# A transformer block on one core: four GpSimd weight scalings and five output stores moved to other places of a hand-written order

## The chip, the cores and the metric

The program runs on one core of one Trainium2 chip. The metric is the device time of one execution in microseconds (us). The kernel before the change was timed three times: median 263.94 us, 263.94 to 264.63. Engines are named as in the profile: PE is TensorE (PEld its weight loads), DVE VectorE, ACT ScalarE, POOL GpSimd, SP SyncE; a q behind the name (SPq, ACTq) means the engine's own instruction queue, where its DMAs are issued.

## What is computed

The block has S = 2048 rows of width D = 448. `c` is one row that modulates both halves. Cut to what matters here:

```
sa, ca, ga, sb, cb, gb = split(silu(c) @ w_mod)
h = layernorm(x) * (1 + ca) + sa
x = x + ga * (linear_attention(h) @ wo)        # 16 heads, softmax feature maps
h = layernorm(x) * (1 + cb) + sb
z = gelu(h @ w_in)                             # 1792 wide
z1, z2 = z[:, :896], layernorm(z[:, 896:])
g = w_sp @ z2 + b_sp                           # 2048 x 2048, over the rows
x = x + gb * ((z1 * g) @ w_out)                # w_out is 896 x 448
```

The gates `ga` and `gb` are multiplied into the rows of `wo` and `w_out` on the chip, once, so that no gate is applied to an output.

## The kernel before, in words

The work is cut into 16 tiles of 128 rows. `fast_path` runs no loops over stages. Instead a string, `ORDER`, lists every step by name, with its tile numbers, its PSUM slot behind `@` and its engine behind `/` (V is DVE, S is ACT, G is POOL, Y is SP). The last loop of `fast_path` (lines 1146 to 1158) reads the string word by word and emits the step. Every engine executes its own instructions in the order in which they were emitted, and waits on semaphores where an operand comes from elsewhere. So the string fixes the order on each engine, and the DMAs of a step marked Y stand in SP's queue in that order too. A PSUM slot (A0, A1, A2 of two banks, B0, B1 of one) is reused only after the last reader of its former content.

The steps that the change and the prediction touch:

- `wos:k` and `wts:k` (`gate_rows`, line 937) multiply one 448-wide row block of `wo` (four blocks, f_wo) or of `w_out` (seven blocks, f_wout) by the gate in f_g_rep, in place. `wts:4`, `wts:3` on POOL and `wts:5` on DVE stay where they are.
- `kP:i` (line 886) normalises the key features, on DVE or POOL; `kA` (line 896) sums keys times values on PE.
- The attention's second half, per tile i: `nM` on PE (numerator and denominator into a slot, line 948), `nX` on ACT and `nC` on DVE (line 959, reads PSUM), then for a pair of tiles `nS` on DVE, three instructions on SBUF data: f_dn add (line 963), its reciprocal (964) and the weights f_w (965). `nT:i` on DVE (968) multiplies the numerator out of PSUM by the weights and is the last reader of the slot; `nA:i` on DVE or POOL (974) adds the two halves into f_opad; `T2` on SP transposes f_opad into f_oT; `wM` and `wN` on PE (984) multiply by `wo`.
- `qM:n` on PE (line 920) makes the query features of the following tiles. `qM:5` takes slot A1 after `nM:0`, so it waits for `nT:0`. `nM:2` takes A0 after `nM:1`, so it waits for `nT:1`.
- `SHw` on PE (767) reads f_win, then `SCw` scales f_win in place, on POOL (773), DVE (775) or ACT (771).
- `T3` on SP (1022) transposes the second LayerNorm's output into f_hT, which `zM` (1028) and `yM` (1056) on PE read; `W` on SP (1064) loads a transposed piece of w_sp.
- `zN:i` (1050) normalises z2, on DVE or POOL; all 16 tiles of it feed `gM` on PE (1072), whose result `gG` on DVE (1078, 1079) joins with z1.
- `oM:t` on PE (1085) multiplies tile t by all seven blocks of f_wout; `oE:t` on DVE (1088) adds x, and `oD:t` on SP (1107) stores 112 KB of output. The last tile, 15, is done in two column parts: `oN`, `oF:15,0` and `oF:15,1` (1100), then `oG:15,0` stored from SP and `oG:15,1` from ACT (1104).

Of the kernel before, what the change touches and what calls it, by code (L numbers as in the profile page):

```python
# [498 lines left out]
T2:0,1 W:0,6 nT:1 SCw:3,1/G SCw:1,1/G SCw:0,2/V SCw:0,3/V SCw:2,1/V nA:1/G T2:1,2 qE:3 qM:4@A2 qM:5@A1 qF:4 qE:4 nM:2@A0 nM:3@A2 nX:2 nC:2 nX:3 nC:3
nS:1 qF:5 nT:2 nT:3 qE:5 wN:0@B0 wR:0/S SB@B1 nM:4@A1 nM:5@A0 bz/S nX:4 nX:5 nC:4 nC:5 nS:2 nA:2/G nT:4 nA:3/G nT:5 nA:4/G wN:1@B0 wQ:0/S wR:1/S  # L500
wQ:1/S SCw:2,0/S l2R:0,2/G l2r:0,2 l2a:0/G SCw:0,0/V nA:5/V T2:2,4 T2:4,6 qM:6@A2 nM:6@A1 nM:7@A0 wN:2@B0 wN:3@B1 qE:6 nX:6 nC:6 nX:7 nC:7 nS:3 nT:6
nT:7 qF:6 wR:2/S wQ:2/S wR:3/S wQ:3/S l2R:2,4/V nA:6/G nA:7/G l2r:2,4 l2a:3/G l2a:2/G qM:7@A2 nM:8@A1 nM:9@A0 wN:4@B0 wM:5@B1 W:1,1 T3:0,1 T2:6,8 qE:7
nX:9 nC:9 nX:8 qF:7 zM:0@A2 wR:4/S gt zG:0 nC:8 l2a:1/V nS:4 nT:8 nT:9 T3:1,2 wR:5/V nM:10@A1 nX:10 wM:6@B0 wQ:4/V wR:6/V SCw:1,0/G SCw:3,0/G wQ:5/S
l2R:4,6/G l2r:4,6 l2a:4/G nM:11@A0 nX:11 nC:10 nC:11 zQ:0/S zM:1@A2 zG:1 zQ:1/S zR:0,2/G zW:0,2 nA:8/V nS:5 nA:9/V nT:10 T3:2,4 wM:7@B0 wR:7/V l2a:5/V
W:1,5 T2:8,10 T3:4,6 yM:0,0@B1 zM:2@A2 zM:3@A1 yG:0,0 wQ:6/S zG:2 zG:3 nT:11 nM:12@A0 nM:13@A2 wQ:7/V zN:0/V zN:1/V nX:12 wM:8@B0 wM:9@B1 nC:12 nX:13
nC:13 zQ:3/S zQ:2/S zM:4@A1 nA:10/V nS:6 wR:8/V nA:11/G nT:12 nT:13 wR:9/V nA:12/V nA:13/V l2R:6,8/G l2r:6,8 l2a:6/G l2a:7/G T2:10,12 wQ:8/S wQ:9/V
zR:2,4/G zW:2,4 yM:0,1@B0 l2R:8,10/G l2r:8,10 l2a:8/G l2a:9/G zG:4 yG:0,1 zQ:4/S zN:2/V zN:3/V zM:5@A0 nM:14@A2 nM:15@A1 wN:10@B0 wN:11@B1 zG:5 nX:14
nX:15 nC:14 nC:15 nS:7 wR:10/S wQ:10/V nT:14 nT:15 nA:14/V nA:15/V wR:11/S zQ:5/S zR:4,6/G zW:4,6 T3:6,8 zM:6@A0 zG:6 wQ:11/S zQ:6/S T2:12,14 W:1,0
wM:12@B0 wM:13@B1 zM:7@A2 l2R:10,12/V yM:0,4@A1 yM:1,4@A0 l2r:10,12 l2a:11/G T3:8,10 T2:14,16 zG:7 zQ:7/S zN:4/V zN:5/V zR:6,8/G zW:6,8 wR:13/V yG:0,4
wQ:13/S zM:8@A2 zM:9@A1 l2a:10/V wR:12/V wM:14@B0 wM:15@B1 wQ:12/V l2R:12,14/V W:1,3 T3:10,12 W:2,1 l2r:12,14 l2a:12/G zN:6/V zN:7/V yG:1,4 zG:8 zG:9  # L510
# [7 lines left out]
guard@A0 gM:1,5@B1 oM:1,0,7@A2 oE:1 oE:2 oE:3 gM:1,2@A0 gG:1,2 gM:1,1@B0 gM:1,3@A2 gM:1,0@A1 gG:1,3 gG:1,0 gM:1,6@A2 oD:0/Y oD:3/Y oD:2/Y gG:1,1
gG:1,5 gG:1,6 gM:2,0@B0 yM:2,2@B1 yG:2,2 W:3,0 W:3,3 W:3,7 W:3,1 W:3,6 W:3,4 W:3,2 gM:2,2@A2 gG:2,0 oM:6,0,7@B0 gM:2,3@B1 oM:4,0,7@A1 gM:2,5@A0 oE:4
gG:2,5 gG:2,3 gM:2,6@A1 gG:2,6 gG:2,2 oM:5,0,7@B1 oE:5 oE:6 gM:2,4@A0 gM:2,1@B0 gG:2,1 oM:7,0,7@B1 oE:7 W:3,5 oD:1/Y gM:3,3@A2 read gG:2,4 oM:8,0,7@B0  # L520
oE:8 oM:10,0,7@B1 oM:9,0,7@B0 oE:9 oE:10 oD:8/Y oD:10/Y oD:6/Y oD:5/Y gM:3,2@A1 gM:3,5@B0 gM:3,1@B1 gG:3,1 gG:3,2 gM:3,6@A0 gM:3,4@B1 gG:3,6 gG:3,4
# [685 lines left out]
```

## Time and profile before

| what | value |
|---|---|
| median of 3 runs | 263.94 us |
| the profiled execution's own time | 263.43 us |
| span of the profiled execution | 261.6 us |
| PE busy | 250.9 us, 96% |
| DVE busy | 158.3 us, 61% |
| POOL busy | 88.9 us, 34% |
| wts and wos on POOL | 6 of 1.16 us, 4 of 1.12 us in the mean |

The span goes from the first to the last instruction in the trace; the execution's own time lies 1.8 us above it. A row of a timeline gives the start, the duration, the engine, the line, the operation, the tiles written and read, and in brackets how long the engine sat idle before it and what ended that. A row that ends in x2 or x8 merges instructions. A matmul's end is modelled and lies a little behind the start of the next. A row of the chain of waits gives start, duration and what the end of the program was waiting for at that moment.

### The profile page before, as it was taken

How to read it: one execution, taken by the hardware profiler on the slowest of the kernel's cores; microseconds unless marked ns; L12 is line 12 of the kernel's file. 1: busy time of each engine (PE TensorE's matmuls, PEld its weight loads, DVE VectorE, ACT ScalarE, POOL GpSimd, SP SyncE). 2: the span in 40 equal slices, each digit the busy share in tenths (PEclk: the TensorE clock that was granted, in tenths of full speed). 3: DMA queues.
4: the chain of work that ended last, by engine and by line, in shares of the span. 5: the costliest groups of instructions: out<-in, count | busy, mean ns of one | idle time of the engine just before them, and what ended most of it. 6: DMA issues, size and time to landing. Idle time of an engine off the chain costs nothing.

```text
span 261.6 us, 4387 instructions
## 1 busy us (share of the span) xinstructions
PE 250.9 (96%) x1654; PEld 136.0 (52%) x1663; DVE 158.3 (61%) x358; ACT 110.1 (42%) x224; POOL 88.9 (34%) x149
## 2 busy tenths in 40 slices
...
GB/s 170 269 295 134 212 136 214 204 249 69 62 120 122 105 131 128 157 154 186 109 3 0 1 0 3 18 3 75 0 3 176 122 0 3 18 105 3 0 38 64
DMA packets 68799, 25.23 MB, mean 96 GB/s; under 512 B 58273, under 2 KB 68642, under 8 KB 68770
## 3 DMA queue, kind: packets, MB, share of 16 engines
...
## 4 chain that ended last, share of the span: by engine, by line
PE 84%; DVE 8%; DMA 3%; issue 1%; POOL 1%; ACT 0%; SPq 0%; DVEq 0%
PE g_ps L1072 37%; PE z_ps L1056 9%; PE o_ps L1085 8%; PE z_ps L1028 8%; PE v_ps L873 4%; PE k_ps L865 4%; DVE f_t L968 3%; PE kvacc L896 3%; PE q_ps L920 3%; PE x_ps L984 3%; DMA f_hT<-f_xpad 2%; DMA f_wq_raw<-in_A_wqkv_dram 2%; PE num L948 2%; PE sh_ps L762 1%; DVE f_dn L963 1%
## 5 line engine op out<-in xcount | busy, mean ns | idle before, releaser
L1072 PEld LDWEIGHTS <-f_z2n 128*128 128x128 bf16 x560 | 50.2, 98 | 46.9
L1078 DVE TENSOR_TENSOR f_gb<-g_ps,f_bsp 128x512 f32<-128x512 f32 (+2 forms) x35 | 20.4, 582 | 55.8 <-PE g_ps L1072 53.6
L1072 PE MATMUL g_ps<-f_Eq,f_z2n 128*128 128x512 bf16 x218 | 49.0, 379 | 0.3
L1059 ACT ACTIVATE f_z1T<-z_ps,f_zb 128x512 bf16<-128x512 f32 x28 | 18.1, 682 | 59.8 <-PE z_ps L1056 59.8
L1028 PE MATMUL z_ps<-f_win,f_hT 112*128 112x448 bf16 (+1 forms) x128 | 26.2, 352 | 0.8 <-DMA f_hT<-f_xpad 0.8
L1056 PE MATMUL z_ps<-f_hT,f_win 112*128 112x512 bf16 x112 | 26.0, 379 | 0.0
L1072 PE MATMUL g_ps<-f_hT,f_z2n 128*128 128x384 bf16 (+1 forms) x224 | 25.1, 272 | 0.0
L1072 PE MATMUL g_ps<-f_wsp,f_z2n 128*128 128x512 bf16 x109 | 24.5, 379 | 0.2
L1085 PE MATMUL o_ps<-f_wout,f_z1T 128*128 128x448 bf16 x105 | 21.7, 352 | 0.1
L1079 DVE TENSOR_TENSOR f_z1T<-f_gb,f_z1T 128x512 bf16<-128x512 f32 (+2 forms) x35 | 20.5, 585 | 1.5
L1088 DVE TENSOR_TENSOR f_xpad<-o_ps,f_x 128x448 bf16<-128x448 f32 x15 | 9.0, 620 | 20.0 <-PE o_ps L1085 20.0
L1028 PEld LDWEIGHTS <-f_hT 112*128 112x128 bf16 (+1 forms) x128 | 12.3, 97 | 13.0 <-DMA f_hT<-f_xpad 1.3
L925 ACT ACTIVATE f_Eq<-q_ps 112x1024 bf16<-112x1024 f32 x16 | 16.1, 1027 | 4.9 <-PE q_ps L920 4.8
L868 ACT ACTIVATE f_E<-k_ps 128x448 bf16<-128x448 f32 x32 | 15.9, 550 | 4.3 <-PE k_ps L865 2.5
L1056 PEld LDWEIGHTS <-f_win 112*128 112x128 bf16 x112 | 10.9, 98 | 12.8
L879 DVE TENSOR_REDUCE f_ksum<-f_E 128x32 f32<-128x896 bf16 x16 | 16.7, 1060 | 0.8 <-ACT f_E L868 0.8
L968 DVE TENSOR_TENSOR f_t<-num,f_w 128x896 bf16<-128x896 f32 x16 | 16.8, 1084 | 0.4
L1032 ACT ACTIVATE f_z2g<-z_ps 128x896 bf16<-128x896 f32 x16 | 14.7, 917 | 4.2 <-PE z_ps L1028 4.0
L920 PE MATMUL q_ps<-f_hT,f_Wq 113*128 113x512 bf16 (+1 forms) x64 | 15.2, 379 | 0.6 <-DVE f_t L968 0.6
L1085 PEld LDWEIGHTS <-f_z1T 128*128 128x128 bf16 x105 | 10.2, 98 | 9.5
L873 PE MATMUL v_ps<-f_wv,f_hT 113*128 113x448 bf16 (+1 forms) x64 | 14.6, 352 | 0.0
L865 PE MATMUL k_ps<-f_Wk,f_hT 113*128 113x448 bf16 (+1 forms) x64 | 14.4, 352 | 0.0
...
## 6 DMA issues: line engine op xcount, KB each, us to landing
out_dram<-f_xpad SPq DMA_DIRECT2D x15, 112.0 KB, 1.8
...
```

What stands on the lines that cost most here:

```text
L865: nc.tensor.matmul(t[:, 0, 0:D], lhsT=hT[0:KR[m], i, m, :], rhs=Wk[0:KR[m], m, :], start=(m == 0), stop=(m == KC - 1))
L873: nc.tensor.matmul(t[:, 0, 0:D], lhsT=hT[0:KR[m], i, m, :], rhs=wv[0:KR[m], m, :], start=(m == 0), stop=(m == KC - 1))
L879: nc.vector.tensor_reduce(out=ksum[:, i], in_=Er[i % NR][:].rearrange("p s (c f h) -> p (s c) h f", c=4, h=HP), axis=AX.X, op=ALU.add)
L920: nc.tensor.matmul(t[:, u, :], lhsT=Wq[0:KR[m], m, cc * CB:cc * CB + P], rhs=hT[0:KR[m], 4 * st:4 * st + 4, m, :], start=(m == 0), stop=(m ...
L968: nc.vector.tensor_tensor(out=tr[i % 2][:], in0=numv(i)[:, :, :, 0:DH], in1=wr[i // 2 % 2][:, i % 2].unsqueeze(3).to_broadcast([P, 2, H, D ...
L1028: nc.tensor.matmul(t[:, hf, 0:D], lhsT=hT[0:KR[m], i, m, :], rhs=win_s[0:KR[m], m, FH + hf * D:FH + (hf + 1) * D], start=(m == 0), stop=(m ...
L1056: nc.tensor.matmul(t[:, 0, :], lhsT=win_s[0:CB, m, fc * P:(fc + 1) * P], rhs=hT[0:CB, 4 * st:4 * st + 4, m, :], start=(m == 0), stop=(m == ...
L1059: nc.scalar.activation(out=stage_b()["z1T"][:, fc, st * 512:(st + 1) * 512], in_=ps["y%d_%d" % (st, fc)][:, 0, :], func=ACT.Gelu_apprx_tan ...
L1072: nc.tensor.matmul(g[:, 0, 0:b - a], lhsT=later["z2n"][:, s_, fc * P:(fc + 1) * P], rhs=wspT[t][:, s_, a:b], start=(s_ == 0), stop=(s_ == ...
L1078: nc.vector.tensor_tensor(out=gb, in0=ps["G%d_%d" % (ch, fc)][:, 0, 0:b - a], in1=bsp[:, t * TCHF + a:t * TCHF + b], op=ALU.add)
L1079: nc.vector.tensor_tensor(out=z, in0=gb, in1=z, op=ALU.mult)
L1085: nc.tensor.matmul(ps["o" + str(t)][:, 0, 0:D], lhsT=later["z1T"][:, fc, t * P:(t + 1) * P], rhs=wout_s[:, fc, :], start=(fc == 0), stop=( ...
```

## The change

Only the string `ORDER` changes. `wts:0`, `wts:6`, `wts:2` and `wts:1` go from between the three `wos` to a place behind `zN:14/G`, much later in POOL's order. `oD:9`, `oD:11`, `oD:12`, `oD:13` and `oD:14` are written further ahead, and `oG:15,0` before `oF:15,1`. All other words keep their order; most of the diff is the string's line breaks. Its core (long lines that only break elsewhere are left out):

```
-kE:13 kS:12 kR:12 kP:12/G kS:13 kR:13 kP:13/G vM:11@B0 vC:11 kA:10@A0 kM:14@B1 kE:14 kF:14 wts:0/G wos:1/G wts:6/G wos:2/G wts:2/G wts:1/G wos:3/G
+kE:13 kS:12 kR:12 kP:12/G kS:13 kR:13 kP:13/G vM:11@B0 vC:11 kA:10@A0 kM:14@B1 kE:14 kF:14 wos:1/G wos:2/G wos:3/G kA:11@A0 kS:14 kR:14 kP:14/V
...
-yM:1,6@B0 yG:0,3 yG:1,6 yM:1,0@A0 yG:1,0 yG:3,6 yM:3,3@A1 yM:0,5@B0 yG:0,5 yG:3,3 yG:0,6 zR:14,16/V zW:14,16 zN:14/G zN:15/V gM:0,6@B1 gM:0,3@B0
+yM:1,6@B0 yG:0,3 yG:1,6 yM:1,0@A0 yG:1,0 yG:3,6 yM:3,3@A1 yM:0,5@B0 yG:0,5 yG:3,3 yG:0,6 zR:14,16/V zW:14,16 zN:14/G wts:0/G wts:6/G wts:2/G wts:1/G
+zN:15/V gM:0,6@B1 gM:0,3@B0 gG:0,3 gM:0,4@A2 gG:0,6 gM:0,2@B0 yM:2,4@B1 yM:2,6@A1 yG:2,6 yG:2,4 gG:0,4 gG:0,2 yM:3,5@A2 yM:3,1@B0 yM:2,3@B1 yG:3,5
...
-gG:3,3 gG:3,5 oD:7/Y gM:3,0@A1 oM:11,0,7@B1 gM:4,2@B0 oD:4/Y gG:3,0 oM:12,0,7@A2 oE:11 oE:12 oM:13,0,7@B1 oE:13 gG:4,2 oD:9/Y gM:4,6@A2 gM:4,4@A1
-gM:4,3@B0 gM:4,0@B1 gG:4,4 gG:4,3 gG:4,0 gM:4,1@A1 gM:4,5@B0 hint oM:14,0,7@B1 gG:4,1 gG:4,6 gG:4,5 oN:15,0@B0 oN:15,1@A1 oE:14 oF:15,0 oF:15,1
-oD:12/Y oD:13/Y oD:14/Y oD:11/Y oG:15,0/Y oG:15,1/S
+gG:3,3 gG:3,5 oD:7/Y gM:3,0@A1 oM:11,0,7@B1 gM:4,2@B0 oD:4/Y gG:3,0 oM:12,0,7@A2 oE:11 oE:12 oD:9/Y oD:11/Y oD:12/Y
+oM:13,0,7@B1 oE:13 oD:13/Y gG:4,2 gM:4,6@A2 gM:4,4@A1 gM:4,3@B0 gM:4,0@B1 gG:4,4 gG:4,3 gG:4,0 gM:4,1@A1 gM:4,5@B0 hint oM:14,0,7@B1 gG:4,1 gG:4,6
+gG:4,5 oN:15,0@B0 oN:15,1@A1 oE:14 oD:14/Y oF:15,0 oG:15,0/Y oF:15,1 oG:15,1/S
```

What it does to POOL's order at the end of the key stage, before and now (line 886 is kP, f_wout rows are wts, f_wo rows wos, line 773 SCw, line 974 nA; a row with x2 or x3 stands for that many):

```order
 L886 TENSOR_TENSOR f_phik<-f_E_129,f_kr_135 128x896
-L937 TENSOR_TENSOR f_wout<-f_wout,f_g_rep 128x448
-L937 TENSOR_TENSOR f_wo<-f_wo,f_g_rep 112x448
-L937 TENSOR_TENSOR f_wout<-f_wout,f_g_rep 128x448
-L937 TENSOR_TENSOR f_wo<-f_wo,f_g_rep 112x448
-L937 TENSOR_TENSOR f_wout<-f_wout,f_g_rep 128x448 x2
-L937 TENSOR_TENSOR f_wo<-f_wo,f_g_rep 112x448
+L937 TENSOR_TENSOR f_wo<-f_wo,f_g_rep 112x448 x3
 L773 TENSOR_SCALAR f_win<-f_win,f_cb_81 112x896 x2
 L974 TENSOR_TENSOR f_opad<-f_t_110 128x4x112
```

Between the last kP and the first SCw there were seven scalings, and now there are three.

POOL's last work of the program, behind the last two `zN` that it executes (f_z2n rows; line 1014 is the power that `zN` needs, line 1119 reads a flag for a branch), as it stands now:

```order
L937 TENSOR_TENSOR f_wout<-f_wout,f_g_rep 128x448
L1014 TENSOR_TENSOR f_zv<-f_zv,f_mhalf 128x2 [waits DVE_49]
L1050 TENSOR_SCALAR f_z2n<-f_z2g_1288,f_zm,f_zv 128x896 [waits DMAHW5_49,Activation_49,Pool_49]
L1014 TENSOR_TENSOR f_zv<-f_zv,f_mhalf 128x2 [waits DVE_49]
L1050 TENSOR_SCALAR f_z2n<-f_z2g_1289,f_zm,f_zv 128x896 [waits Activation_49,Pool_49]
L937 TENSOR_TENSOR f_wout<-f_wout,f_g_rep 128x448 x4
L1119 TENSOR_LOAD flag [waits DVE_49]
```

The four scalings are new there; before, the flag read came right behind the last f_z2n row. The four have no wait of their own.

The last stores in SP's queue. Of the words of the string only `oD:11` changes its place among SP's own instructions: the sequence was 9, 12, 13, 14, 11, then `oG:15,0`, and is now 9, 11, 12, 13, 14, then `oG:15,0`. The rows name no tile, so the change shows only in their waits (line 1107 is oD, line 1104 oG):

```order
 L1107 DMA out_dram<-f_xpad 128x448 [waits DMAHW2_49,DVE_49]
 L1107 DMA out_dram<-f_xpad 128x448 [waits DMAHW3_49,DVE_49]
-L1107 DMA out_dram<-f_xpad 128x448 [waits DMAHW4_49]
+L1107 DMA out_dram<-f_xpad 128x448 [waits DMAHW4_49,DVE_49]
 L1104 DMA out_dram<-f_xpad 128x256 [waits DMAHW5_49,DVE_49]
```

The last `oD` row was tile 11's, which needed no wait for DVE behind tile 14's; it is now tile 14's, which waits for its own `oE:14`. SP issues as many stores as before.

More of the change, by code (lines that the diff above doesn't have):

```diff
@@ L499 @@
[L499 to L510, printed above, removed]
@@ L511 @@
-zQ:8/S W:1,4 zM:10@A2 zM:11@A1 zQ:9/S zR:8,10/G zW:8,10 zG:10 zG:11 zQ:11/S wR:14/V l2a:13/V T3:12,14 W:2,3 W:2,7 wR:15/V wQ:14/V wQ:15/V l2R:14,16/V
+kE:13 kS:12 kR:12 kP:12/G kS:13 kR:13 kP:13/G vM:11@B0 vC:11 kA:10@A0 kM:14@B1 kE:14 kF:14 wos:1/G wos:2/G wos:3/G kA:11@A0 kS:14 kR:14 kP:14/V
+vM:12@B0 kM:15@A2 vC:12 kF:15 kE:15 vM:13@B1 vC:13 kA:12@A0 kS:15 kR:15 kP:15/V vM:14@B0 kA:13@A0 vM:15@B1 vC:14 vC:15 kA:14@A0 csB@B0 kA:15@A0 esB
+KV:0/V KV:1/V KZ:0 KZ:1 qM:3@A2 ccB@B0 nM:0@A1 nM:1@A0 ecB qF:3 nX:0 SHw:3@B0 SHw:2@B1 nX:1 nC:0 nC:1 nS:0 nT:0 nA:0/V T2:0,1 W:0,6 nT:1 SCw:3,1/G
@@ new lines @@
+SCw:1,1/G SCw:0,2/V SCw:0,3/V SCw:2,1/V nA:1/G T2:1,2 qE:3 qM:4@A2 qM:5@A1 qF:4 qE:4 nM:2@A0 nM:3@A2 nX:2 nC:2 nX:3 nC:3 nS:1 qF:5 nT:2 nT:3 qE:5
+wN:0@B0 wR:0/S SB@B1 nM:4@A1 nM:5@A0 bz/S nX:4 nX:5 nC:4 nC:5 nS:2 nA:2/G nT:4 nA:3/G nT:5 nA:4/G wN:1@B0 wQ:0/S wR:1/S wQ:1/S SCw:2,0/S l2R:0,2/G
+l2r:0,2 l2a:0/G SCw:0,0/V nA:5/V T2:2,4 T2:4,6 qM:6@A2 nM:6@A1 nM:7@A0 wN:2@B0 wN:3@B1 qE:6 nX:6 nC:6 nX:7 nC:7 nS:3 nT:6 nT:7 qF:6 wR:2/S wQ:2/S
+wR:3/S wQ:3/S l2R:2,4/V nA:6/G nA:7/G l2r:2,4 l2a:3/G l2a:2/G qM:7@A2 nM:8@A1 nM:9@A0 wN:4@B0 wM:5@B1 W:1,1 T3:0,1 T2:6,8 qE:7 nX:9 nC:9 nX:8 qF:7
@@ new lines @@
+zM:0@A2 wR:4/S gt zG:0 nC:8 l2a:1/V nS:4 nT:8 nT:9 T3:1,2 wR:5/V nM:10@A1 nX:10 wM:6@B0 wQ:4/V wR:6/V SCw:1,0/G SCw:3,0/G wQ:5/S l2R:4,6/G l2r:4,6
+l2a:4/G nM:11@A0 nX:11 nC:10 nC:11 zQ:0/S zM:1@A2 zG:1 zQ:1/S zR:0,2/G zW:0,2 nA:8/V nS:5 nA:9/V nT:10 T3:2,4 wM:7@B0 wR:7/V l2a:5/V W:1,5 T2:8,10
+T3:4,6 yM:0,0@B1 zM:2@A2 zM:3@A1 yG:0,0 wQ:6/S zG:2 zG:3 nT:11 nM:12@A0 nM:13@A2 wQ:7/V zN:0/V zN:1/V nX:12 wM:8@B0 wM:9@B1 nC:12 nX:13 nC:13 zQ:3/S
+zQ:2/S zM:4@A1 nA:10/V nS:6 wR:8/V nA:11/G nT:12 nT:13 wR:9/V nA:12/V nA:13/V l2R:6,8/G l2r:6,8 l2a:6/G l2a:7/G T2:10,12 wQ:8/S wQ:9/V zR:2,4/G zW:2,4
@@ new lines @@
+yM:0,1@B0 l2R:8,10/G l2r:8,10 l2a:8/G l2a:9/G zG:4 yG:0,1 zQ:4/S zN:2/V zN:3/V zM:5@A0 nM:14@A2 nM:15@A1 wN:10@B0 wN:11@B1 zG:5 nX:14 nX:15 nC:14
+nC:15 nS:7 wR:10/S wQ:10/V nT:14 nT:15 nA:14/V nA:15/V wR:11/S zQ:5/S zR:4,6/G zW:4,6 T3:6,8 zM:6@A0 zG:6 wQ:11/S zQ:6/S T2:12,14 W:1,0 wM:12@B0
+wM:13@B1 zM:7@A2 l2R:10,12/V yM:0,4@A1 yM:1,4@A0 l2r:10,12 l2a:11/G T3:8,10 T2:14,16 zG:7 zQ:7/S zN:4/V zN:5/V zR:6,8/G zW:6,8 wR:13/V yG:0,4 wQ:13/S
+zM:8@A2 zM:9@A1 l2a:10/V wR:12/V wM:14@B0 wM:15@B1 wQ:12/V l2R:12,14/V W:1,3 T3:10,12 W:2,1 l2r:12,14 l2a:12/G zN:6/V zN:7/V yG:1,4 zG:8 zG:9 zQ:8/S
@@ L512 @@
+W:1,4 zM:10@A2 zM:11@A1 zQ:9/S zR:8,10/G zW:8,10 zG:10 zG:11 zQ:11/S wR:14/V l2a:13/V T3:12,14 W:2,3 W:2,7 wR:15/V wQ:14/V wQ:15/V l2R:14,16/V
 yM:1,2@B0 zM:12@A2 zM:13@A1 yG:1,2 zG:12 yM:1,3@B0 yM:0,2@B1 yM:2,1@A2 yM:2,5@A0 zQ:10/V zN:8/V zN:9/V zR:10,12/V l2r:14,16 l2a:14/V l2a:15/V zG:13
```

14 lines of the change are left out of this document (6 added, 8 removed).

## The prediction

> **What bounds the kernel now.** I read the page's busy line and its chain by engine first, then the chain of waits in order of time, then the timelines of DVE, POOL and PE side by side where the chain leaves PE, and at last the stores at the end.
>
> ```profile
> PE 250.9 (96%) x1654; PEld 136.0 (52%) x1663; DVE 158.3 (61%) x358; ACT 110.1 (42%) x224; POOL 88.9 (34%) x149
> ...
> PE 84%; DVE 8%; DMA 3%; issue 1%; POOL 1%; ACT 0%; SPq 0%; DVEq 0%
> ```
>
> PE does most of the time on the chain and the change takes no work from it. A gain can come only where the chain is elsewhere: 8% on DVE, 3% on DMA, and what follows the last matmul. The chain of waits leaves PE for DVE once, for a long stretch:
>
> ```profile
> 56.24 0.88 PE num L948 x16
> 57.14 0.20 ACT f_Sx L956
> 57.36 0.20 DVE f_cr L959
> ...
> 79.63 0.59 PE num L948 x8
> ```
>
> From 57.36 to 79.63 us DVE, not PE, is late nearly everywhere; this is the first division by the denominators, and POOL's seven moved or kept scalings end just there. DVE's timeline of it:
>
> ```profile
> 57.59 0.80 DVE L963 TENSOR_TENSOR f_dn<-f_cr 128x32 f32<-128x32 f32 x1
> 58.81 1.01 DVE L965 TENSOR_TENSOR f_w<-f_Sx,f_dn 128x64 f32<-128x64 f32 x1
> 59.85 1.09 DVE L968 TENSOR_TENSOR f_t<-num,f_w 128x896 bf16<-128x896 f32 x1
> 60.98 0.39 DVE L974 TENSOR_TENSOR f_opad<-f_t 128x448 bf16<-128x448 bf16 x1
> 61.29 1.08 DVE L968 TENSOR_TENSOR f_t<-num,f_w 128x896 bf16<-128x896 f32 x1
> 64.23 0.19 DVE L963 TENSOR_TENSOR f_dn<-f_cr 128x32 f32<-128x32 f32 x1
> 64.84 0.23 DVE L965 TENSOR_TENSOR f_w<-f_Sx,f_dn 128x64 f32<-128x64 f32 x1
> 67.42 0.93 DVE L963 TENSOR_TENSOR f_dn<-f_cr 128x32 f32<-128x32 f32 x1
> ```
>
> The same add of 128x32 numbers takes 0.19 us at 64.23 and 0.80 at 57.59 and 0.93 at 67.42; the weights take 0.23 or 1.01. POOL's rows at the slow ones:
>
> ```profile
> 57.31 1.02 POOL L937 TENSOR_TENSOR f_wo<-f_wo,f_g_rep 112x448 bf16<-112x448 bf16 x1
> 58.73 1.01 POOL L773 TENSOR_SCALAR f_win<-f_win,f_cb 112x896 bf16<-112x896 bf16 x1 [0.39 <-PE sh_ps L767]
> 66.27 2.03 POOL L974 TENSOR_TENSOR f_opad<-f_t 128x448 bf16<-128x448 bf16 x2 [2.78 <-DVE f_t L968]
> ```
>
> POOL's instructions end at 58.33, 59.74 and 68.30; DVE's slow ones end at 58.39, 59.82 and 68.35. So a DVE instruction with two SBUF operands, issued while a POOL instruction runs, ends 0.05 to 0.08 us behind it: it waits for POOL. f_t, with one operand in PSUM, takes its 1.09 and 1.08 beside POOL and does not wait.
>
> **The change, first place: the key stage's end.** `wos:3` stood last of seven scalings and ended at 58.33. With four gone before it, POOL's work behind kP ends about four scalings earlier, near 54.4, and POOL then waits for PE's sh_ps, which frees SCw at 58.73 as now (its bracket names PE). So f_dn finds POOL idle at 57.59: 0.80 - 0.19 = 0.61 saved. f_w then starts at 58.20 and ends at 58.43, before SCw starts at 58.73: 1.01 - 0.23 = 0.78 saved. `nT:0` ends at 59.55 in place of 60.94, 1.39 earlier. What is late next is PE:
>
> ```profile
> 58.46 1.90 PE L920 MATMUL q_ps<-f_hT,f_Wq 113*128 113x512 bf16 x8
> 61.00 1.91 PE L920 MATMUL q_ps<-f_hT,f_Wq 113*128 113x512 bf16 x8 [0.64 <-DVE f_t L968]
> 62.74 1.00 PE L948 MATMUL num<-f_KVbd,f_Eq 112*128 112x120 bf16 x16
> 65.86 1.00 PE L948 MATMUL num<-f_KVbd,f_Eq 112*128 112x120 bf16 x16 [0.39 <-ACT f_Eq L925]
> ```
>
> `qM:5` at 61.00 idles 0.64 us for `nT:0`. That idle goes, and no more: `qM:4`'s eight matmuls must be through. From start to start eight of them take 62.74 - 61.00 = 1.74, so `qM:5` may come at 58.46 + 1.74 = 60.20, 0.80 earlier. The gain here is therefore 0.64 to 0.80 of the 1.39, and I take 0.7. `nM:2` follows `qM:5` at 62.0 and needs `nT:1`, and with it `nX:2`, DVE's next `nC` and every later pair move up together. `nT:1` is behind `nA:0`, which has two SBUF operands and comes at 59.6, while the first SCw runs to 59.74. f_w was let in between the two SCw at 59.74 in the row above, so I let `nA:0` in there too: it ends at 60.1 and `nT:1` at 61.2, in time. If it has to wait for the second SCw too, to 60.74, `nT:1` ends near 62.1, and the gain is 0.55. The transposition behind `nA:0` is no limit either:
>
> ```profile
> 61.40 1.19 SPq L847 DMA_TRANSPOSE f_oT<-f_opad  x1
> ...
> f_oT<-f_opad SPq DMA_TRANSPOSE x1, 2.4
> ```
>
> It lands 2.4 us after 61.40, at 63.8, just when `wN:0` now needs it; from 60.1 it lands at 62.5, from 61.1 at 63.5, and 0.3 of waiting there would be lost in the 0.39 that PE waits at 65.86 anyway. From 62 to 79.63 every instruction of the chain waits on the one before, on PE, DVE, ACT and POOL alike, so the shift arrives at PE's long busy stretch. Bounds: 0.8 above; below, 0 if the shift is used up on the way, by more waiting for POOL elsewhere.
>
> **Second place: behind the last zN.** Four scalings, uncontended, cost what `wts:3` costs:
>
> ```profile
> 114.25 1.03 POOL L937 TENSOR_TENSOR f_wout<-f_wout,f_g_rep 128x448 bf16<-128x448 bf16 x1
> 125.26 1.32 POOL L1050 TENSOR_SCALAR f_z2n<-f_z2g,f_zm,f_zv 128x896 bf16<-128x896 bf16 x1
> 137.43 0.69 DVE L1078 TENSOR_TENSOR f_gb<-g_ps,f_bsp 128x512 f32<-128x512 f32 x1 [11.73 <-PE g_ps L1072]
> ...
> 163.14 2.81 PE o_ps L1085 x14
> ```
>
> 4 x 1.03 = 4.1 us from 126.58 to 130.7. DVE is idle from 125.70 to 137.43, so nothing waits for POOL there. The first reader of these blocks is o_ps at 163.14, 32 us later; the new wait of its matmuls on POOL is met long before. Behind the four on POOL stands only the flag read, which waits for a DVE result of the late program. Cost 0; without that cover, had they ended after 163.14, their whole lateness would count.
>
> **Third place: the end.** The last rows of the timeline, with the times to landing of a store that is alone (the one issued at 249.31) and of the last two:
>
> ```profile
> 249.31 0.33 SPq L1107 DMA_DIRECT2D out_dram<-f_xpad  x1
> ...
> 255.35 0.62 DVE L1088 TENSOR_TENSOR f_xpad<-o_ps,f_x 128x448 bf16<-128x448 f32 x1 [0.55 <-PE o_ps L1085]
> 256.00 1.32 SPq L1107 DMA_DIRECT2D out_dram<-f_xpad  x2
> 256.11 0.43 DVE L1100 TENSOR_TENSOR f_xpad<-o_ps,f_x 128x256 bf16<-128x256 f32 x1
> 256.69 0.36 DVE L1100 TENSOR_TENSOR f_xpad<-o_ps,f_x 128x192 bf16<-128x192 f32 x1 [0.15 <-PE o_ps L1096]
> 257.08 0.38 ACTq L1104 DMA_DIRECT2D out_dram<-f_xpad  x1
> 257.42 0.38 SPq L1104 DMA_DIRECT2D out_dram<-f_xpad  x1
> ...
> out_dram<-f_xpad SPq DMA_DIRECT2D x1, 112.0 KB, 1.7
> ...
> out_dram<-f_xpad SPq DMA_DIRECT2D x1, 64.0 KB, 2.7
> ...
> out_dram<-f_xpad ACTq DMA_DIRECT2D x1, 48.0 KB, 2.5
> ```
>
> SP issues tile 14's store at 256.00 and tile 11's behind it, so `oG:15,0`, ready at 256.54, is issued at 257.42 and lands at 257.42 + 2.7 = 260.12, the last event but the closing 1.5 us of the span. ACT's half lands at 257.08 + 2.5 = 259.58. Now tile 11's store goes ahead of tile 12's, and `oG:15,0` can be issued at 256.6, 0.85 earlier; it lands at 259.3 at its 2.7. Then ACT's half is last, at 259.58: a gain of 0.54. It will also land sooner, since 112 KB less is under way; at the lone store's 1.7 it would land at 258.78, a gain of 1.34. I take 0.75, nearer to the row of the same store. Below: if the half lands as late as 3.0 after issue, nothing is gained.
>
> The Trainium skill (DMA: Bandwidth & Descriptors, Anatomy of one DMA) puts a transfer at about 2.0 us fixed plus its bytes over 436 GB/s, fitted on another issue path. By it ACT's 48 KB land 2.1 us after issue, the last term would be 0.94, and the sum 1.64; it would also give a lone 112 KB store 2.26 us, where the trace shows 1.7, so I stay with the rows.
>
> **The sum.** 0.7 + 0 + 0.75 = 1.45 us. The profiled execution took 263.43 us with a span of 261.6; it comes to 261.98 (span 260.15). The median of the runs lies 0.51 above the profiled one: 263.94 - 1.45 = 262.5 us. Bounds of this case: 0.55 + 0.54 = 1.1 to 0.8 + 1.34 = 2.1, so 261.8 to 262.85.
>
> **The rivals.**
>
> *The first stage gives nothing*: f_dn and f_w are short again, but the shift is eaten by later waits between DVE and POOL, as the one at 67.42. For it: nine tenths of a microsecond can go by one bad overlap. Against: the later POOL steps wait for the same DVE results and move with them. 263.94 - 0.75 = 263.2.
>
> *The end gives nothing*: the landing of ACT's half grows to 3 us. For it: with `oG:15,0` just ahead, both compete. Against: fewer bytes compete than now. 263.94 - 0.7 = 263.2.
>
> *Both, or no waiting for POOL at all*: the change does not do what it seems to. 263.9.
>
> *Slower: the transpositions.* PE waits for a DMA once in its long stretch:
>
> ```profile
> 112.14 3.22 PE L1028 MATMUL z_ps<-f_win,f_hT 113*128 113x448 bf16 x16 [0.80 <-DMA f_hT<-f_xpad]
> ...
> 104.49 2.67 SPq L1064 DMA_TRANSPOSE f_Eq<-in_B_w_sp_dram  x2
> ...
> DMA to landing us min/median/max: 2.6/3.1/4.3
> ```
>
> `T3:10,12`, issued at 107.75 behind two pieces of w_sp, took 4.3 against a median of 3.1. If the shifted stage puts it in the way of two more such pieces, it lands 2.67 later, and each microsecond goes straight onto PE: 263.94 - 1.45 + 2.67 = 265.2. It decides from a landing of 2.24 us later on: 1.45 to come out even and 0.79 for a slowdown that shows. Against: SP's order is written, and everything on it here waits for results that shift together.
>
> **How the numbers follow.** 0.3% of 263.94, 0.79 us, is about what a measurement of this kernel can tell from no change: faster is below 263.15, slower above 264.73. My case has 0.60 (all of it faster), the first rival 0.08, the second 0.12, the third 0.10 (all three within the bound), the last 0.10 (slower). So faster 0.60, same 0.30, slower 0.10. The range takes in the first four cases: 261.8 to 264.0.
>
> **What would show it.** Right: f_dn at 57.6 near 0.19 and f_w near 0.23, PE's idle of 0.64 before the second q_ps gone, the later rows of the chain 0.7 earlier up to 79 us; four f_wout rows on POOL from about 126 us, DVE idle beside them; only one 112 KB store issued after 255 us and SP's `oG:15,0` issued ahead of ACT's. Wrong: an f_opad or f_w row of DVE at 58 to 62 us that is as long as before, a longer wait than 0.80 for f_hT near 111 us, or an ACT half that lands 3 us after its issue.

## The result, and the profile after

The changed kernel takes 262.42 us in the median of 20 runs (261.27 to 263.80), beside 263.64 us for the kernel before in 20 runs on the same chip (262.14 to 265.05): ratio 0.9957, 95% interval 0.9940 to 0.9975. By the ratio that is 1.13 us, with an interval from 0.66 to 1.58 (the two medians lie 1.22 apart); the prediction had 1.45. Run again beside three other kernels it took 262.44 us, ratio 0.9967 (0.9948 to 0.9985), 0.87 us. The sum came out, but not both of its terms: the first place gave 0.8 us, and the last gave nothing that the times can tell from zero.

The profiled execution after the change is a long one. Its own time is 263.80 us, the highest of its 20, and its span of 262.0 us is above the 261.6 of the profile before. So the two spans tell nothing here, and the stages have to be compared one by one, each from its own start.

First VectorE and GpSimd at the start of the divisions, in the changed kernel (start, duration, engine, line, operation, tiles, in brackets the idle time before it and what ended that):

```profile
58.42 0.19 DVE L963 TENSOR_TENSOR f_dn<-f_cr 128x32 f32<-128x32 f32 x1
...
59.04 0.22 DVE L965 TENSOR_TENSOR f_w<-f_Sx,f_dn 128x64 f32<-128x64 f32 x1
59.30 1.09 DVE L968 TENSOR_TENSOR f_t<-num,f_w 128x896 bf16<-128x896 f32 x1
60.42 0.40 DVE L974 TENSOR_TENSOR f_opad<-f_t 128x448 bf16<-128x448 bf16 x1
...
67.47 0.93 DVE L963 TENSOR_TENSOR f_dn<-f_cr 128x32 f32<-128x32 f32 x1
```

```profile
50.44 3.40 POOL L937 TENSOR_TENSOR f_wo<-f_wo,f_g_rep 112x448 bf16<-112x448 bf16 x3
59.57 2.13 POOL L773 TENSOR_SCALAR f_win<-f_win,f_cb 112x896 bf16<-112x896 bf16 x2 [5.73 <-PE sh_ps L767]
```

GpSimd is idle from 53.84 to 59.57. f_dn takes 0.19 us where it took 0.80, and f_w 0.22 where it took 1.01. `nA:0` at 60.42 came in between the two scalings of f_win, after 0.4 us of work and no wait that shows, as the prediction had assumed. The other slow f_dn, at 67.47, still waits for `nA` on GpSimd; the change does not touch it.

PE in the same stretch of the changed kernel:

```profile
56.94 1.00 PE L948 MATMUL num<-f_KVbd,f_Eq 112*128 112x120 bf16 x16
...
59.29 3.63 PE L920 MATMUL q_ps<-f_hT,f_Wq 113*128 113x512 bf16 x16
62.76 1.03 PE L948 MATMUL num<-f_KVbd,f_Eq 112*128 112x120 bf16 x16
```

The two groups of eight query matmuls have become one row of 16, with no idle time between. From the start of `nM:0` to the start of `nM:2` it is 62.76 - 56.94 = 5.82 us, where it was 62.74 - 56.10 = 6.64. The shift stays to the end of the stretch in which VectorE is late: the row of eight num matmuls that the prediction's chain has at 79.63 starts 23.53 us behind `nM:0` before the change and 23.52 in b_stores (below), and 22.73 to 22.76 in the profiles of the changed kernel, of a_scalings, c_changed_again, d_sp_last, f_fill_set and k_long_fill.

The new place of the scalings, and the wait for the transposition, in the changed kernel:

```profile
126.94 4.00 POOL L937 TENSOR_TENSOR f_wout<-f_wout,f_g_rep 128x448 bf16<-128x448 bf16 x4
```

```profile
112.53 3.22 PE L1028 MATMUL z_ps<-f_win,f_hT 113*128 113x448 bf16 x16 [1.15 <-DMA f_hT<-f_xpad]
```

The four take 4.00 us at 126.94. The idle before PE's z_ps is 1.15 us here and was 0.80: 0.35 of the stage's gain is lost again in this execution.

The end of the changed kernel, timeline and then SP's waits (engine and line, what it waited for, us in total, times, longest):

```profile
256.39 0.33 SPq L1107 DMA_DIRECT2D out_dram<-f_xpad  x1
...
256.96 0.70 SPq L1104 DMA_DIRECT2D out_dram<-f_xpad  x1
257.08 0.36 DVE L1100 TENSOR_TENSOR f_xpad<-o_ps,f_x 128x192 bf16<-128x192 f32 x1 [0.15 <-PE o_ps L1096]
257.47 0.38 ACTq L1104 DMA_DIRECT2D out_dram<-f_xpad  x1
```

```profile
out_dram<-f_xpad SPq DMA_DIRECT2D x1, 64.0 KB, 2.7
out_dram<-f_xpad ACTq DMA_DIRECT2D x1, 48.0 KB, 2.4
```

```profile
SPq L1202 <- ACTq L1174: 0.7, 1, 0.7
```

SP's half is issued ahead of ACT's now. It lands at 256.96 + 2.7 = 259.66, and ACT's at 257.47 + 2.4 = 259.87, so the last landing comes 2.79 us behind the start of the last VectorE add (257.08); before it was 260.12 - 256.69 = 3.43. The stores did land 0.64 earlier, within the 0.54 to 1.34 of the prediction's third place. But from that last add to the end of the span it is 262.0 - 257.08 = 4.92 us, and it was 261.6 - 256.69 = 4.91. The last row says why: at the close SP waits 0.7 us for ACT.

How each engine closes is seen at line 1174, the branch over the general path. First the kernel before, then the changed one (engine, instruction, count: duration in ns, first and last start):

```profile
L1174 SPq EVENT_SEMAPHORE  x8: 17/17/17, 258.4 to 260.3; - x8
...
L1174 ACTq COMPARE_BRANCH  x1: 54/54/54, 257.5 to 257.5; - x1
...
L1174 ACTq EVENT_SEMAPHORE  x1: 17/17/17, 260.5 to 260.5; - x1
```

```profile
L1174 SPq EVENT_SEMAPHORE  x8: 17/17/17, 258.2 to 260.0; - x8
...
L1174 ACTq COMPARE_BRANCH  x1: 54/54/54, 257.9 to 257.9; - x1
...
L1174 ACTq EVENT_SEMAPHORE  x1: 17/17/17, 261.1 to 261.1; - x1
```

ACT starts its jump as soon as its store is issued and signals 3.0 us later (257.5 to 260.5 before, 3.2 after). SP's last semaphore comes 0.1 to 0.2 us behind the last landing. Before, the two closed 0.2 us apart, and the end came 1.3 us after SP's and 1.1 after ACT's. Now SP's comes at 260.0, but ACT's only at 261.1, and the end is 0.9 behind that. ACT's store is issued after the same add as before, so its jump is where it was.

### The profile page after: what moved, and what is told of

Read it like the earlier page. It is cut to its first block, busy times and chain, and to the rows that moved or that the text cites. A ratio compares the mean times of both kernels' runs of the same rounds, so it can differ in the third digit from the quotient of the medians.

```text
span 262.0 us, 4397 instructions
## 1 busy us (share of the span) xinstructions
PE 251.7 (96%) x1663; PEld 137.4 (52%) x1663; DVE 157.2 (60%) x358; ACT 110.1 (42%) x224; POOL 88.8 (34%) x149
## 4 chain that ended last, share of the span: by engine, by line
PE 76%; DVE 9%; DMA 7%; POOL 4%; issue 2%; SPq 0%; ACT 0%; DVEq 0%; POOLq 0%
PE g_ps L1072 37%; PE z_ps L1056 9%; PE z_ps L1028 8%; PE o_ps L1085 8%; DMA f_hT<-f_xpad 3%; DMA f_wout<-in_B_w_out_dram 3%; PE x_ps L984 3%; POOL f_xpad L842 3%; DVE f_t L968 2%; PE q_ps L920 2%; PE num L948 2%; DMA f_wq_raw<-in_A_wqkv_dram 2%; PE tps L808 1%; PE k_ps L865 1%; PE v_ps L873 1%
```

## The experiments

The theory after the result: (1) the gain is the first place alone, a VectorE instruction with two SBUF operands waiting for a GpSimd instruction that runs; (2) the stores land earlier, but ACT's jump to the end, begun behind its store, takes the place of the landing. Rivals: the stores gave part of the gain; the last landing sets the end; the four scalings held up something else at their old place; the long first profile shows a cost of the change.

**Scalings alone.** The kernel before, with only the four words moved:

```
-wts:0/G wos:1/G wts:6/G wos:2/G wts:2/G wts:1/G wos:3/G
+wos:1/G wos:2/G wos:3/G
...
-zN:14/G zN:15/V
+zN:14/G wts:0/G wts:6/G wts:2/G wts:1/G zN:15/V
```

> The four scalings moved, the stores as before. My reason (DVE's f_dn and f_w wait for GpSimd's scalings): f_dn near 0.19 us and f_w near 0.23, PE's idle of 0.64 us before the second q_ps gone, 0.7 to 0.8 us off the time, about 262.9 against 263.6 before. Rival (the stores bring nothing, the scalings all of the measured 1.2): about 262.4.

Measured: 262.20 us, ratio 0.9966 (0.9948 to 0.9983). Its PE:

```profile
55.78 1.00 PE L948 MATMUL num<-f_KVbd,f_Eq 112*128 112x120 bf16 x16
...
58.13 3.63 PE L920 MATMUL q_ps<-f_hT,f_Wq 113*128 113x512 bf16 x16
61.61 1.03 PE L948 MATMUL num<-f_KVbd,f_Eq 112*128 112x120 bf16 x16
```

The stage takes 5.83 us. As far as the intervals tell, this half alone has the whole gain of the change.

**Stores alone.** The changed kernel with the four words put back (and gone from behind `zN:14/G`):

```
-wos:1/G wos:2/G wos:3/G
+wts:0/G wos:1/G wts:6/G wos:2/G wts:2/G wts:1/G wos:3/G
```

> The stores moved, the scalings as before. My reason (the last landing ends the program, and tile 11's store stood ahead of it): 0.5 to 0.75 us off, about 263.0. Rival (the span ends 4.0 us behind ACT's store, by ACT's own jump to the end of the program, whatever SP does): within 0.2 us of before, 263.4 to 263.6.

Measured: 263.04 us, ratio 0.9995 (0.9971 to 1.0020). Rows of DVE, of PE and of the close:

```profile
57.18 0.80 DVE L963 TENSOR_TENSOR f_dn<-f_cr 128x32 f32<-128x32 f32 x1
```

```profile
60.59 1.91 PE L920 MATMUL q_ps<-f_hT,f_Wq 113*128 113x512 bf16 x8 [0.64 <-DVE f_t L968]
```

```profile
L1174 SPq EVENT_SEMAPHORE  x8: 17/17/17, 257.6 to 259.3; - x8
...
L1174 ACTq EVENT_SEMAPHORE  x1: 17/17/17, 260.0 to 260.0; - x1
```

f_dn and PE's idle of 0.64 are as before the change. SP's last semaphore comes 259.3 - 256.27 = 3.03 us behind the start of the last add (3.61 before), and ACT's 3.73 behind it (3.81 before). The landings moved and ACT's close hardly did, and the time shows no gain. The interval is wide, though: it reaches from 0.76 us faster to 0.53 slower, so it does not exclude the predicted 0.75 by itself. The closing rows of all profiles, gathered below, say more.

**Last store from SP.** The changed kernel with

```
-oG:15,1/S
+oG:15,1/Y
```

> The changed kernel, with the very last store (48 KB) issued from SP behind SP's 64 KB and not from ACT, so that ACT has nothing left to do at the end. If the last landing ends the program: that store is issued some 0.3 us later than now and lands later, so 0.2 to 0.4 us slower than the changed kernel, about 262.7. If ACT's jump behind its store ends it: 0.4 to 0.8 us faster than the changed kernel, about 261.8; DVE's own jump behind its last add is then the next in line.

Measured: 261.99 us, ratio 0.9962 (0.9945 to 0.9979). Its closing rows:

```profile
L1174 SPq EVENT_SEMAPHORE  x8: 17/17/17, 257.5 to 258.4; - x8
...
L1174 ACTq COMPARE_BRANCH  x1: 50/50/50, 195.1 to 195.1; - x1
L1174 ACTq EVENT_SEMAPHORE  x1: 17/17/17, 198.3 to 198.3; - x1
```

ACT jumps at 195 us, long ahead of the end, and needs its 3.2 us there too. The end comes 259.8 - 255.68 = 4.12 us behind the start of the last add, 0.8 less than in the changed kernel's first profile and 0.7 less than in its second. The time does not tell it apart from the changed kernel by itself: 0.9962 against 0.9957 and 0.9967.

**Two pieces of w_sp behind the transposition.** The changed kernel with `W:2,1` and `W:1,4` moved behind `T3:12,14`:

```
-W:1,3 T3:10,12 W:2,1 ... W:1,4 ... T3:12,14
+W:1,3 T3:10,12 ... T3:12,14 W:2,1 W:1,4
```

> The changed kernel, with two loads of w_sp (W:2,1 and W:1,4) moved behind the transposition T3:12,14 in SP's queue. If that transposition is late because it shares the way with them (it landed 4.3 us after issue before the change and 4.7 after it, the median 3.1): it lands near 3.1, PE's idle of 0.80 (before) and 1.15 us (after) at 112 us is gone, about 1 us faster than the changed kernel, 261.4. If it is late by itself: no change from 262.4.

Measured: 262.19 us, ratio 0.9969 (0.9948 to 0.9990). The idle for f_hT near 111 us is gone, and a new one stands six microseconds later:

```profile
117.36 3.21 PE L1028 MATMUL z_ps<-f_win,f_hT 113*128 113x448 bf16 x16 [0.74 <-ACT f_z1T L1059]
```

PE comes earlier to a slot that ACT has not yet read, and waits there as long as it had waited for the transposition (0.74 against 0.80 before the change).

**The changed kernel again**, unaltered.

> The changed kernel, unaltered, beside the three others of this call. Every theory expects what it had before: a ratio to the kernel before near 0.996, 262.4 us, within its own spread of about 1 us either way. In its profile f_dn at the first division takes 0.19 us and the stage from the start of nM:0 to the start of nM:2 on PE takes 5.82 us, as in the first profile of it. The start of nM:0 shall lie nearer to 56.1 than to 56.94 if the late start of that profile was chance, and near 56.9 again if the change brings it.

Measured: 262.44 us, ratio 0.9967 (0.9948 to 0.9985); the stage is 62.31 - 56.49 = 5.82 us. The start of `nM:0`, 56.49, lies halfway, so this run alone does not settle why the first profile began its stage late. All of them do: in the five profiles whose order is the changed kernel's up to there (after, a_scalings, c_changed_again, d_sp_last, h_w_behind) `nM:0` starts at 56.94, 55.78, 56.49, 56.06 and 55.68 us, and in the two with the old order at 56.10 and 55.70. The start varies from execution to execution, and not with the change.

Part of it is again a wait between VectorE and GpSimd. In the first profile of the changed kernel GpSimd's wos began at 50.44, just ahead of `kP:14` on VectorE:

```profile
50.63 1.32 DVE L886 TENSOR_TENSOR f_phik<-f_E,f_kr 128x896 bf16<-128x896 bf16 x1
```

```profile
54.38 0.59 PE L896 MATMUL kvacc<-f_vaug,f_phik 128*128 128x116 bf16 x8 [0.63 <-DVE f_phik L886]
```

In the profile before, the same instruction took 0.62, and it does so in c_changed_again: VectorE had come first there.

**Four scalings of nothing at the old place.** The changed kernel with a new step behind `wos:3` (line numbers behind it are 3 higher from here on):

```
+    def fil(k):
+        nc.gpsimd.tensor_tensor(out=zero[:, 0:D], in0=zero[:, 0:D], in1=g_rep[:, 1, :], op=ALU.mult)
...
-wos:3/G
+wos:3/G fil:0 fil:1 fil:2 fil:3
```

> The changed kernel with four extra multiplications of 128x448 on GpSimd, of a tile of zeros, at the place from which the four scalings were taken; the scalings themselves stay late, and the extra four belong to no result. Theory (the gain of the first place comes only from GpSimd being idle when the divisions start): f_dn takes 0.80 us again, f_w 1.0, PE idles 0.64 before the second group of query matmuls, the stage takes 6.6 us, and the time is that of the stores moved alone, ratio 0.9995, about 263.2 us. Rival (the gain comes from something else that the four scalings did at their old place, such as a semaphore wait of o_ps or of the wos behind them): the stage stays at 5.8 us and the time at 262.4.

Measured: 262.40 us, ratio 0.9981 (0.9957 to 1.0004). DVE, then POOL:

```profile
57.23 0.19 DVE L966 TENSOR_TENSOR f_dn<-f_cr 128x32 f32<-128x32 f32 x1
...
57.85 0.58 DVE L968 TENSOR_TENSOR f_w<-f_Sx,f_dn 128x64 f32<-128x64 f32 x1
...
59.59 1.03 DVE L977 TENSOR_TENSOR f_opad<-f_t 128x448 bf16<-128x448 bf16 x1
```

```profile
53.98 4.36 POOL L940 TENSOR_TENSOR f_zero<-f_zero,f_g_rep 128x448 bf16<-128x448 bf16 x4
58.38 2.01 POOL L773 TENSOR_SCALAR f_win<-f_win,f_cb 112x896 bf16<-112x896 bf16 x2
```

The expectation failed by a hair's breadth in time: f_dn came at 57.23, where the third extra scaling had ended and the fourth, which starts at 57.3, had not begun. It slipped through. f_w came at 57.85 and ended at 58.43, behind the end of the extra work at 58.34, and `nA:0` ended at 60.62, 0.23 behind the two scalings of f_win. So the wait is there, on two other instructions, but up to `nM:2` the stage lost only 0.1 us (61.68 - 55.75 = 5.93). More of the loss shows at the end of the stretch in which VectorE is late, here and then in c_changed_again:

```profile
78.81 0.59 PE L951 MATMUL num<-f_KVbd,f_Eq 112*128 112x120 bf16 x8
```

```profile
79.22 0.60 PE L948 MATMUL num<-f_KVbd,f_Eq 112*128 112x120 bf16 x8
```

That is 78.81 - 55.75 = 23.06 us behind `nM:0`, against 79.22 - 56.49 = 22.73 for the changed kernel and 23.53 before: the extra scalings brought back 0.33 of the 0.80. The time is no more than unclear.

**Memsets at the old place.** The same step with another body, six times:

```
+        nc.gpsimd.memset(junk2[:], 0.0)
```

> As the run before, but the extra work at the old place is six memsets of 128x896 on GpSimd, which keep that engine busy over the start of the divisions and read nothing. First theory (any instruction that runs on GpSimd holds back a VectorE instruction with two SBUF operands): f_dn 0.5 to 0.8 us, the stage 6.2 to 6.6, time about 263.2. Second theory (only one that reads SBUF does): f_dn 0.19 and f_w 0.23 beside a busy GpSimd, and then the stage 5.8 and time about 262.4, unless the memsets last past 58.7 us and hold up the scalings of f_win behind them. The Trainium skill (SBUF — State Buffer, section on the two separate sides) has the second rule for the case of two SBUF inputs; no run of this case has shown it so far.

Measured: 261.99 us, ratio 0.9958 (0.9936 to 0.9980); the profiled execution is its longest, 263.37. DVE, then POOL:

```profile
58.76 0.19 DVE L966 TENSOR_TENSOR f_dn<-f_cr 128x32 f32<-128x32 f32 x1
...
59.37 0.23 DVE L968 TENSOR_TENSOR f_w<-f_Sx,f_dn 128x64 f32<-128x64 f32 x1
...
60.75 0.39 DVE L977 TENSOR_TENSOR f_opad<-f_t 128x448 bf16<-128x448 bf16 x1
```

```profile
55.49 5.36 POOL L940 MEMSET f_junk<- 128x896 bf16 x6
```

GpSimd is busy from 55.49 to 60.85, over the whole of f_dn and f_w and the first 0.1 us of `nA:0`, and none of the three is held up: the stage takes 63.10 - 57.27 = 5.83 us. So a busy GpSimd is not enough; what the scalings do and the memsets do not is to read SBUF. The Trainium skill (SBUF — State Buffer, SBUF: two separate sides) says that a VectorE instruction with two SBUF inputs contends for the port pair that it shares with GpSimd "only against a GpSimd op that reads SBUF", and that whichever of the two starts first keeps the pair for its whole instruction while the other waits. These rows agree with the first; the slow f_dn and f_w of the kernel before, which end 0.06 and 0.08 us behind GpSimd's instruction, agree with the second.

In the same profile a VectorE instruction that reads one tile and a column of scalars is held up as well, beside a GpSimd instruction that reads SBUF (VectorE, then GpSimd):

```profile
63.25 1.02 DVE L775 TENSOR_SCALAR f_win<-f_win,f_cb 112x896 bf16<-112x896 bf16 x1
```

```profile
62.99 1.03 POOL L977 TENSOR_TENSOR f_opad<-f_t 128x448 bf16<-128x448 bf16 x1
```

It takes 0.44 us in the other profiles, and here 1.02. So the wait is not a matter of two tiles alone.

**A longer instruction over f_dn.** The step as one memset and two multiplications of 128x896 (line numbers 6 higher):

```
+        if k == 0:
+            nc.gpsimd.memset(junk2[:], 0.0)
+        else:
+            nc.gpsimd.tensor_tensor(out=junk2[:], in0=junk2[:], in1=junk2[:], op=ALU.mult)
```

> The changed kernel with other extra work on GpSimd at the old place: one memset of 128x896 and then two multiplications of 128x896 of a scratch tile, which belong to no result. In e_fill_scal f_dn began at 57.23 us, 0.07 us ahead of the fourth extra scaling, and slipped through; here the last extra instruction is 1.65 us long and stands over the start of f_dn whatever the jitter. Theory (a VectorE instruction with two SBUF operands waits for the GpSimd instruction that runs when it comes, if that reads SBUF): f_dn takes 0.7 to 1.1 us, f_w 0.6 to 1.1 behind the first scaling of f_win, the stage takes 6.4 to 6.8 us, PE idles 0.5 to 0.8 before the second group of query matmuls, and the time is 263.0 to 263.4. Rival (the lock is real but costs the program little, since later waits make up for it): the rows as in the theory, the stage 6.4 or more, and the time still 262.4.

Measured: 262.59 us, ratio 0.9986 (0.9967 to 1.0005).

```profile
58.59 0.19 DVE L969 TENSOR_TENSOR f_dn<-f_cr 128x32 f32<-128x32 f32 x1
```

```profile
54.87 3.44 POOL L943 TENSOR_TENSOR f_junk<-f_junk 128x896 bf16<-128x896 bf16 x2
```

A miss again: in the profiled execution `nM:0` began at 57.11, f_dn at 58.59, and the extra work had ended at 58.31. "Whatever the jitter" was wrong, since GpSimd's work did not move with PE. The profile tells nothing on the theory. Neither this run nor the one with four scalings brought the whole loss back in a profile, and the latter only 0.33 us of it; the kernel before and b_stores have it all.

**The wos later, and the last store from SP.** The changed kernel with `oG:15,1/Y` and

```
-kF:14 wos:1/G wos:2/G wos:3/G
+kF:14
...
-kP:15/V
+kP:15/V fil:15 wos:1/G wos:2/G wos:3/G
```

where `fil:15` on GpSimd copies one column of what `kP:15` wrote.

> The changed kernel with two edits: the last store goes through SP and not ACT, as in d_sp_last, and GpSimd's three wos wait until VectorE has done kP:15 (by a copy of one column of its result). Theory (the wos at 50.4 us held back kP:14 in one profile, 1.32 us in place of 0.62, and PE lost 0.63 us): kP:14 and kP:15 take 0.56 to 0.62 us each, PE does not wait for f_phik at 54 us, the wos run from about 53 to 56.7 us and are done before f_dn starts, and the end from the last VectorE add is near 4.1 us: ratio 0.993 to 0.995, 261.5 to 261.8 us. Rival (the overlap of kP:14 and the first wos happens in few executions, so that nothing is left to gain): as d_sp_last, ratio 0.996, 262.0 us. Against both: if the wos begin so late that they reach f_dn, f_dn takes 0.5 to 0.8 us again and the time is 262.6 or more.

Measured: 261.62 us, ratio 0.9944 (0.9923 to 0.9966). `kP:14` and `kP:15` take 0.63 and 0.62 us, and the wos are done before f_dn comes at 57.20:

```profile
53.20 3.01 POOL L937 TENSOR_TENSOR f_wo<-f_wo,f_g_rep 112x448 bf16<-112x448 bf16 x3
```

From the last add (255.46) to the end (259.6) it is 4.14 us.

**The wos later alone**, with the last store on ACT.

```
-oG:15,1/Y
+oG:15,1/S
```

> The changed kernel with GpSimd's three wos behind kP:15 and the last store on ScalarE as in the change: one half of i_sp_wos_late. If the late wos bring what i_sp_wos_late had beyond d_sp_last: kP:14 and kP:15 at 0.62 us, ratio 0.995, 262.0 us. If nearly all of the gain of i_sp_wos_late was the last store on SP: the same two rows, but a time of 262.2 to 262.4, as the changed kernel, with 4.6 to 4.9 us from the last VectorE add to the end.

Measured: 262.26 us, ratio 0.9966 (0.9945 to 0.9986), with `kP:15` at 0.62. That is the changed kernel's time: the late wos alone bring nothing that these runs can tell.

**All three edits**: i_sp_wos_late with the two pieces of w_sp behind the transposition.

```
-W:1,3 T3:10,12 W:2,1 ... W:1,4 ... T3:12,14
+W:1,3 T3:10,12 ... T3:12,14 W:2,1 W:1,4
```

> i_sp_wos_late with the two pieces of w_sp behind T3:12,14 as in h_w_behind: the last store on SP, the wos behind kP:15, and no transposition of f_hT behind pieces of w_sp near 108 us. If the idle of 0.7 us at f_hT is worth its length: 261.0 us, ratio 0.991 to 0.992. If the wait for the slot that ScalarE frees takes its place, as in the profile of h_w_behind: 261.6, ratio 0.994, PE idle 0.5 to 0.8 for ACT near 115 us in place of the wait for f_hT.

Measured: 261.74 us, ratio 0.9947 (0.9928 to 0.9967), no better than without the pieces moved. The idle near 111 us is gone, and it is back at the next transposition:

```profile
117.51 3.21 PE L1031 MATMUL z_ps<-f_win,f_hT 113*128 113x448 bf16 x16 [1.00 <-DMA f_hT<-f_xpad]
```

**One activation behind ACT's store.** The changed kernel with a last step on ACT:

```
+    def fil(k):
+        nc.scalar.activation(out=junk[:], in_=junk[:], func=ACT.Square)
...
-oG:15,1/S
+oG:15,1/S fil:0
```

> The changed kernel with one more activation of 128x896 on ScalarE behind the last store that ScalarE issues; nothing waits for its result. The same shape takes 0.95 us elsewhere in this kernel. Theory (the end is set by the engine whose jump over the general path starts last, here ScalarE behind its store, and not by the landing of the last store): ScalarE's branch starts 0.95 to 1.0 us later, its closing semaphore comes 0.95 to 1.0 later, the span and the time grow by that, 263.4 us, and from the last VectorE add to the end it is 5.6 us in place of 4.6 to 4.9. Rival (the landing of the last store sets the end): the activation is done before the store has landed, and the time stays at 262.4.

Measured: 262.50 us, ratio 0.9973 (0.9952 to 0.9994): the time of the changed kernel. Timeline, then the closing rows:

```profile
257.04 0.95 ACT L940 ACTIVATE f_junk<-f_junk 128x896 bf16<-128x896 bf16 x1 [61.21 <-DVE f_xpad L1103]
```

```profile
L1177 SPq EVENT_SEMAPHORE  x8: 17/17/17, 257.5 to 259.0; - x8
...
L1177 ACTq COMPARE_BRANCH  x1: 54/54/54, 257.1 to 257.1; - x1
...
L1177 ACTq EVENT_SEMAPHORE  x1: 17/17/17, 259.7 to 259.7; - x1
```

The theory as it was written failed: the activation starts at 257.04 and would end at 257.99, but the branch starts at 257.1. ACT's queue goes on to the jump while the engine works, so the activation lay under the jump and pushed nothing back. With that the run does not tell the two theories of the end apart, since the jump was not delayed; SP still waited 0.3 us for ACT at the close.

What the runs show of the end, taken together. In the three profiles with both halves on SP the end lies 1.3 to 1.4 us behind SP's closing semaphore, and so it does in the two with the stores as before the change (the kernel before and a_scalings), where it lies 1.1 and 1.0 us behind ACT's. In the nine with the new order of the stores and the last one on ACT it lies 0.9 us behind ACT's each time, and 1.5 to 2.3 us behind SP's. In eight of these nine SP waits for ACT at the close, 0.2 to 0.9 us, and in none of the other five. So the landing did come last before the change, but by little: by 0.1 to 0.2 us, an estimate from these distances. Once the landing moved, ACT's close was the last. With both halves on SP it is VectorE's closing semaphore that comes last, at 258.4 to 258.6 us, 0.1 to 0.2 us behind SP's.

From the start of the last VectorE add to the end it is 4.91 and 4.64 us with the stores as before, 4.38 to 5.04 (4.63 in the mean) in the nine, and 4.12 to 4.24 with both halves on SP. In the times this shows less sharply. The three with both halves on SP have 261.99, 261.62 and 261.74 us, and the changed kernel, its repetition and g_wos_late 262.42, 262.44 and 262.26. The 17 runs of i_sp_wos_late and m_all against the 24 of c_changed_again and g_wos_late, which were timed beside them, differ in the median by 0.67 us, with a 95% interval (resampled runs) from 0.08 to 1.01; but d_sp_last differs by only 0.2 us from a_scalings and h_w_behind, which were timed beside it with the last store on ACT (262.20 and 262.19).

## Why the prediction was right or wrong

*What bounds the kernel now* was read rightly: the change takes nothing off PE's work, and the gain came where the chain leaves it.

*The change, first place*: right in mechanism, at its upper bound. f_dn and f_w lost the durations that were worked out (0.61 and 0.78), the idle of 0.64 went, and `qM:5` became limited by `qM:4`, as the prediction said. Taken were 0.7 us, measured 6.64 - 5.82 = 0.82 in the two profiles and 6.63 - 5.83 = 0.80 between the kernels with only the one half and only the other. The whole shift arrived at PE's long busy stretch, as the prediction argued: 23.53 us from `nM:0` to the num row at its start became 22.73. a_scalings is 0.34% (0.17 to 0.52) faster, 0.9 us. The rule that was read from the rows ("it waits for POOL") was too wide in one respect, which this kernel could not show: f_fill_set has a GpSimd that runs and is not waited for. In another it was too narrow: an instruction with one tile of SBUF data can wait too.

*Second place*: right. The four scalings take 4.00 us where VectorE is idle, and cost nothing.

*Third place: the end*: the step that failed. "The last event but the closing 1.5 us of the span" was the landing, and the prediction let the end follow the landing wherever it went. The landing did come earlier, by 0.64 us from the last add (SP's semaphore 0.58 in b_stores). But 0.2 us behind SP's semaphore stood ACT's, 3.0 us of jump after the issue of its store, and the change moved nothing on ACT; the prediction put ACT's own close at nothing. The term of 0.75 was worth 0.1 to 0.2 by the closing rows, and nothing that the times show: 0.9995 (0.9971 to 1.0020) for the stores alone. The prediction's own rival for this, that the half would land 3 us after its issue, is not what happened either: it landed 2.4 us after. The estimate by the Trainium skill (DMA: Bandwidth & Descriptors, Anatomy of one DMA) decided nothing either: it gave 2.1 us for the 48 KB, and the runs show 2.2 to 2.6 from ACT and 1.8 to 2.2 from SP.

*The sum*: 262.5 us predicted and 262.42 measured, and this is in part luck. The base was the first three runs, whose median of 263.94 lies 0.30 above that of all 20. With the end at zero the sum would have been 263.1 from that base, and 262.8 from the median of the 20. The measured gain of 1.13 us (0.66 to 1.58) holds both 0.82, for the first place alone, and 1.45, so the time by itself could not have shown that a term failed.

*The rivals*: "the end gives nothing" came true, or nearly, for another reason than the one it gave, and its time of 263.2 was not the one measured. "Slower: the transpositions" did not, but it touched something real: PE's wait for f_hT near 111 us is between 0.44 and 1.15 us in the twelve profiles that keep SP's order, 1.15 in the changed kernel's first profile, which is above the 0.80 that the prediction had named as a sign of being wrong, and 0.61 in its second. It also held a mistake in the name: the transposition issued at 107.75 behind two pieces of w_sp is `T3:12,14`, not `T3:10,12`, as the words in the order string show. The working does not depend on the name.

*What stays open*: what the jump of about 3 us consists of (ACT needs 2.6 to 3.3 us for it, whether it is late or at 195 us; an instruction queue of the DMA engines, q14, moves data inside it, between 196 and 197 us in d_sp_last and between 258 and 259 in the changed kernel, but no run shows that ACT waited for that), and what sets the length of the wait for `T3:12,14`. Moving pieces of w_sp out of its way replaced it by another wait, twice. No run of extra GpSimd work brought back the whole 0.8 us at the old place.
